# Retabling a hand-ordered attention and FFN kernel: DMA issue times and held buffers in the planner, and a masked product for the row maxima

## The chip, the cores and the metric

One core of one Trainium2 chip runs the whole program. The time is device microseconds of one launch; three runs of the kernel before gave 1584.69, 1585.31 and 1585.92 us, median 1585.31. One more execution was taken by the hardware profiler and took 1585.88 us.

## The reference

Four batches of 12416 rows with 128 channels go through an induced-set attention block, and each resulting row through a SwiGLU FFN (d_model 128, d_ff 1536). Everything is FP32.

```python
def mab(q, kv):
    s = scale * (q @ kv.transpose(0, 2, 1))
    s = s - s.max(-1, keepdims=True)
    a = np.exp(s)
    a /= a.sum(-1, keepdims=True) + 1e-09
    return a @ kv
h = mab(I, x)                 # 32 inducing points attend to all rows of the batch
x = mab(x, h)                 # every row attends to the 32 results
rms = np.sqrt(np.mean(x * x, axis=-1, keepdims=True) + 1e-06)
xn = x / rms * rms_g
g = xn @ w_gate
silu = g * (1.0 / (1.0 + np.exp(-g)))
val = xn @ w_val
return (silu * val @ w_out).astype(np.float32)
```

## The kernel before

**Slots.** A batch is cut into 7 sets of rows (`per`): six of four "units" (512 rows wide, the sixth 480) and a last one of a single unit of 256. That makes 25 units, and a unit has 12 blocks of d_ff. One pass through `slot` handles one block of one unit, so a batch has 300 slots and the kernel 1200. A slot is called k (0 to 299 in its batch) below. In a slot TensorE computes a gate product (L751) and a value product (L762) into PSUM banks, ScalarE applies silu (L759), and VectorE multiplies the two (L768).

**Three kinds of output product.** The product with `wo` is accumulated in `acc` at L688, and the letter of the slot in the table `letters` says how it is made. A "." slot uses full FP32, which the compiler issues as two matmuls (`acc<-u,wo`). An "s" or "d" slot splits the number in halves and makes three reduced-precision matmuls (L709, L711, L688: `u<-xn,xn`, `u<-xn,more`, `acc<-xn,more`; `project3`). The split itself costs other engines time. "s" (sums): one ScalarE pass (L733), one VectorE pass (L734), one GpSimd pass (L743). "d" (differences): two ScalarE passes (L737, L742) and two GpSimd passes (L738, L743), none on VectorE. The tiles that hold the halves are called `xn`, `sg`, `sv` or `xT` after the buffers that they borrow.

**Other work is threaded between the slots.** While batch b goes through its FFN, the attention of batch b+1 is computed: transposes, scores (L342) with their running maxima, exponentials, the sum over rows (`sum_h`, L396), then `stack` (L475) and `place` (L484). `stack(i)` multiplies the gate or value weights by the 32 attention results and leaves the rounded half in a tile `whi` (ScalarE, L478) and the rest in `wlo` (VectorE, L479). `place(i, k)` then copies three stripes of a half into the stacked weights `sg` or `sv` by DMA on the SP queue: k = 0 and 1 read `whi`, k = 2 and 3 read `wlo`. A "seam" prepares the attention weights of the next set of the current batch: `turn_a`, `square` (L521), `turn_z` (L527, L528), `scale`, `root`, `apply`, `turn_b`, `split` (L552, L555). `gather` (L567) then copies its result into the moving operand of the next unit by DMA, also on SP. So are the loads and the result's stores (L725).

**The order is written out by hand, in tables that a search found.** `letters` gives the kind of each slot; `places` the slot of each threaded step; `ordered` where the output products of earlier slots are issued (p: full, t: split); `banks` which of five PSUM banks each product takes; `workers` which of three buffers `work0` to `work2` each scratch tile takes; `holders` which of nine buffers each product tile takes. A scratch tile (`eT`, `z`, `aT`, `e`, `whi`, `wlo`) takes its buffer from the list in turn:

```python
def worker(shape, dtype, name):
    return work.tile(shape, dtype, name=name, tag=f"work{works.pop(0)}")
```

The buffer of `whi` or `wlo` is free for its next holder only when the last DMA of `place` that reads it has landed. The engines run their own instruction streams in order; SP too issues its DMAs in order.

**The maxima of batches 1 to 3.** After the scores of a batch, `max1` reduces seven maxima per partition to one, `max2` transposes them onto one partition, takes the maximum over the four quarters there and scales it, and `max3` spreads it back with a matmul and copies it to `nbias`. Batch 0 has its own start-up order (`first`), which does this by a masked product (L843, L851, L854).

Of the kernel before, what the change touches and what calls it, by code (L numbers as in the profile page):

```python
# [9 lines left out]
F32 = mybir.dt.float32  # L10
# [4 lines left out]
ALU = mybir.AluOpType  # L15
AX = mybir.AxisListType
PSUM = bass.MemoryType.PSUM

P = 128
R = 4  # L20
# [3 lines left out]
def kernel(  # L24
# [45 lines left out]
    nc = tc.nc  # L70
    B, N, C = x.shape
    m = inducing.shape[0]
# [10 lines left out]
    NS = len(per)  # L83
# [226 lines left out]
    def attention(b, load_next):  # L310
# [38 lines left out]
        def max1():  # L349
            mx = st["mx"] = small.tile([P, 1], F32, name="mx")  # L350
            nc.vector.reduce_max(out=mx[:], in_=st["gmx"][:], axis=AX.X)

        def max2():
            ps = bank()
            nc.tensor.transpose(ps[0:1, 0:P], st["mx"][:], ident[:])
            row = once.tile([1, m], F32, name="row")
            nc.vector.reduce_max(out=row[:], in_=ps[0:1, 0:P].rearrange("p (q m) -> p m q", m=m), axis=AX.X)
            row4 = st["row4"] = once.tile([P, P], F32, name="hg")[0:1, :].rearrange("p (q m) -> p q m", m=m)
            nc.vector.tensor_scalar_mul(out=row4, in0=row[:].unsqueeze(1).to_broadcast((1, R, m)), scalar1=-SCALE)

        def max3():
            ps = bank()
            nc.tensor.matmul(ps[:, 0:1], st["row4"].rearrange("p q m -> p (q m)"), ones[0:1, 0:1],
                             start=True, stop=True)
            nbias = st["nbias"] = small.tile([P, 1], F32, name="nbias")
            nc.vector.tensor_copy(out=nbias, in_=ps[:, 0:1])
# [681 lines left out]
    def given(b, k, u, j):  # L1048
# [4 lines left out]
        ..........................ss..ssdd.....sss.dsd..sd.ssdsds...d.sdddsd.....sdsdsss.s....sdsdsdss..ssss  # L1053
        dsdssd..dsd..ssdd...sd.sssd.ds....ss..dssd..sssdsssssd..ddsss.ssss..ssdsssssss..sss.ssssdd..ssssdsds
        sd..sssdd.s.ss..sssssssds...sss.ssssdd...ssssssd.s....ssd.d.ss..sssssd.d....ss.ss.sss...sssd.sdsdd..
        """,
        """
        d...dsssss..dssssdsd.s..dd.sd.sd.s..ssd.ss.dss..sds.sddsss..sdd...ds.d..ssss.d.dsd...ssssdsssd..ssd.
        sd.dss..sd.sssdsd...sssdsd.dsd..ss....dssd..ssssdssssd..ssdssssd.s..ssssdssssd...s.sdsssds..ssssdsds
        dd..sssssss..d..s.s.sssssd..sssssds.ds..ssssd.d.sd....s..dsssd..ssss.dsd....sss..sssss...s.sssdsdd..  # L1060
        """,
        """
        s.ssdsd.ds..ssssdsd.s...ss.s..dssd..sdsssds.ss..ssdsd..dd...sddss.dsds..s.s.sssds...sdsss.sdds..sssd
        ssdd.s..sssd.ssds...sssdssdsds.....s.d.sdd..sss.sssssd..sdssssdd.s..sss.dsssss..sssd.sssds..dsssdsss
        ds..ssd.sds.sd..sss.ssssss..d.sd.sssss..ssssssssds......dd..ss..sssd.ds.ss...s.sssssd...s.s.sd.dsd..
        """,
        """
        s.s.ssssd.s.sssssd.sds.sss...d..ssd..ssssdsd..ssss.ssssssdd..sss..sss..ssssssdsssss.s.sssd.s.sssss.s
        dsd.sssssd.s..ds.s.sssssd.s.d..ss.ssss.sd.ssssssssds.ssd..ssdsss..s..sss..sssdssssssdsd..ss.ssssss.s
        dsss.dsd.s..s.sssssss..sdsssss.sss.dss.sss.sssdsd.s.sdssss...s.sssss...sssdss.ds.sdsdsss..ssss...d..  # L1070
# [4 lines left out]
        0 0 1 1 2 2 2 2 3 3 4 4 4 5 6 6 7 7 8 8 9 9 10 10 11 11 11 11 12 12 13 13 13 13 13 14 16 17 18 16 19 18 20   # L1075
        21 16 20 21 21 22 22 24 23 25 24 27 24 24 27 27 24 28 29 24 28 29 30 30 31 32 32 32 34 34 35 35 35 35 35 39 
        41 39 42 43 44 45 47 49 51 54 54 54 55 58 59 62 62 55 65 65 62 66 64 67 66 70 71 66 70 73 73 77 75 77 77 79 
        85 81 84 85 86 89 87 89 90 92 92 96 97 97 96 100 103 103 104 108 108 109 101 116 109 111 111 110 116 110 118 
        123 116 129 120 132 123 132 134 135 136 136 142 146 147 148 148 154 148 160 161 151 162 153 156 159 168 163 
        168 171 171 174 175 178 191 192 196 197 198 198 199 208 199 203 205 210 212 208 215 197 208 216 216 218 202   # L1080
        213 202 215 206 215 208 215 211 221 227 215 221 218 225 230 233 227 230 239 239 233 239 247 248 239 239 250 
        245 250 251 254 254 255 256 257 256 256 256 260 263 266 262 269 268 268 271 277 273 275 275 280 281 285 287 
# [3 lines left out]
        0 0 6 12 4 13 18 13 20 18 18 21 19 24 26 30 27 30 36 35 35 36 39 39 42 46 48 54 50 52 54 58 60 60 66 62 53   # L1086
        63 59 66 63 70 65 69 71 74 72 87 75 81 76 83 79 79 87 82 93 96 97 100 103 118 100 102 108 107 100 114 103 
        104 111 118 115 122 130 119 132 126 133 134 135 136 136 142 146 147 148 146 156 149 160 161 151 162 153 159 
        164 169 164 166 171 178 174 175 180 180 185 195 196 198 198 198 204 201 202 202 211 214 204 209 198 204 209 
        214 219 202 215 202 215 208 204 209 215 212 218 221 216 221 215 220 226 234 227 233 237 239 233 233 240 246   # L1090
        239 244 246 245 249 251 254 254 255 256 257 256 256 256 257 263 266 262 269 269 268 270 271 272 272 275 277 
        281 281 283 287 293 299 
        """,
        """
        0 0 6 12 5 7 18 8 20 22 22 24 31 24 27 28 33 30 36 35 36 36 38 38 42 48 48 50 51 53 54 55 57 60 66 60 58 64 
        63 66 63 67 65 67 68 71 72 93 74 80 82 83 86 87 93 93 99 101 97 105 103 120 105 111 108 115 100 117 104 104 
        112 120 118 124 129 121 132 124 128 134 135 136 136 136 146 147 148 158 158 158 160 161 162 162 162 165 166 
        168 163 164 169 172 174 175 178 180 188 196 197 197 198 198 197 198 200 202 201 203 203 206 206 203 207 211 
        212 210 204 210 207 214 219 215 223 220 228 219 225 228 232 235 229 237 241 229 248 249 229 253 253 254 254 
        255 256 256 256 256 258 260 262 264 269 270 267 275 276 280 285 288   # L1100
        """,
        """
        2 4 6 19 21 21 25 26 31 35 37 53 58 58 60 62 76 78 81 103 108 108 110 113 125 129 131 156 158 158 161 161 
        173 177 181 199 206 206 209 215 218 225 227 250 253 253 257 257 264 269 271 
# [3 lines left out]
        ;;;,pp;,,,p;,p;,p;;,pp;;,pp;;;,pp,,,p;;,p;;,p;;,p;;,p;;;p;;;,p;;,pp;,pp;,pp;,tt;,pp;,,t;,t;;,p;;,tp;;,tp;;,p;,  # L1108
        pt;,tp;;,tp;;,t;;,tp;;,tp;;,tt;;,tt;;,tp;;,tp;;,t;,tp;;;,t;,tt;,pp;,t;;,pp;;,pt;;,t;,,p;;,t;,ppt;;,tt;;,tt;;,t
        p;;,tt;,,p;;,t;,pt;,t;;,pt;t;;,tp;;,tt;,p;;,t;,tt;;,tt;,tp;;,tp;,t;,t;;,tp;;,t;,tp;,t;,t;;,t;;,t;,p;;,t;,pp;,p  # L1110
        ;;,tp;,t;;,t;;,tt;,pt;,pp;,tt;,pp;,t;;,tp;,p;,t;;;t;;,t;,tp;;,tt;;t;t,t;,tt;,t;;,tp;;,,t;,t;;,t;,p;,pp;,t;,tt;
        ;,tt;;,tt;,p;,tp;,t;;t;,tt;,t;,t;;,t;;,tp;,t;;,t;,t;,tp;,t;,t;,,ttp;;;,tp;;,tp;,t;,t;,t;,t;,t;,t;;,tp;;,t;,tp;
        ,t;,t;;,tt;;,p;,t;,p;;,t;,t;,t;,tp;,t;,t;,tp;,t;,t;;,tt;;,p;;,t;,tp;;,t;,t;,tp;,t;,t;;,tt;;,t;,p;;,tp;,t;,t;,t
        ;;,tt;;,t;;,pp;,tt;,pp;,pp;,tp;;,tp;,t;;,p;,t;;,pp;,t;,t;,t;,tt;;t;,p;;,t;,p;;,tp;,t;,p;;,pp;,t;,t;,pt;;,t;;,t
        t;;,tp;,p;;,t;,t;,t;,pt;,t;;,pt;;,tp;,tp;,t;;,p;,tp;;,tp;;,t;,t;;;,tt;,t;,pt;;,tt;;,tt;;;p,p;;,t;;p;t,p;,t;,tp
        ;;,p;,t;,pt;;,t;,tt;;,pt;;,t;,pp;;,tt;;,tp;;,t;;,tp;,tt;;,tp;;,t;,tt;,tp;;;,t;;tt,t;;,tp;,p;,tt;;,tp;;,t;;,t;;
        ,pp;,p;,t;,pt;;,tp;,tt;,pp;;,t;;t;,tp;;,t;,p;,tt;,t;,tp;;,t;,t;,t;;,t;p;,tp;;,t;,tt;,tp;,t;,p;;,t;;,t;,t;,p;,t
        ;,pt;;,t;,t;,t;;,p;;,tp;;,t;,pt;,p;,t;,t;,t;;,p;,t;,tp;,tp;,tp;,tp;;,tp;,t;,t;,p;;,t;;t;;,tt;,p;;,tt;;t;t,tt;;
        ,tt;;,tp;;,t;;t,tt;;,tp;;,t;,t;,t;;,pp;,pt;,tp;,t;;;t;,tt;,t;;,t,,tt;;;,t;,p;,tp;;,t;,tp;,tp;,t;;,t;;,t;,tp;,t
        ;,pt;,t;,t;,tt;;,t;;,,t;;,t;,t;,t;,pt;,t;,t;,t;,pp;;,tt;;;,tp;;,tp;,p;;,tt;;pp,t;,t;,t;;;t;,tp;,t;,pt;,t;,t;;,  # L1120
        t;,t;;t,p;;,tp;,t;,t;,t;;,t;,t;;,t;,p;,t;;,pp;,tp;,tp;,tp;;;p,tp;,p;,t;,t;;,t;;,tp;,t;;,t;,tt;;,tp;,tp;;,t;,p;
        ;,pp;;,t;;,tp;,t;,t;,t;p,p;,t;;,t;;,t;,t;,p;,tt;;,tp;,t;;,tp;;,t;,tp;,tp;,pp;;,,tt;;,tt;;,t;,p;;,t;,p;,t;,tp;;
        ,t;,tt;;,tp;;,tt;;,tp;;,t;;,pp;;,t;,tt;,pp;;;,tt;;,tp;;,tp;,pt;;,tt;,t;;,tp;;,t;,,t;,t;;,t;,pp;,t;;,t;,tt;;,tp
        ;;,tp;;;,t;,pp;;,tt;,tt;,t;;,p;,p;,tp;;,t;,p;,t;,t;,pt;,tt;;,t;,t;;,p;,tt;;,pt;,pp;;,tt;;;t;,tt;;,t;,p;,t;,tp;
# [116 lines left out]
```

## Time and profile before

| what | value |
|---|---|
| median of three runs | 1585.31 us |
| profiled execution | 1585.88 us |
| its span, first to last instruction | 1584.0 us |
| TensorE busy | 1565.6 us |
| VectorE busy | 1458.7 us |
| ScalarE busy | 1300.0 us |
| GpSimd busy | 1428.0 us |
| granted TensorE clock | 0.999 |

The span lacks 1.9 us of the profiled execution's time. Busy times of different engines overlap. TensorE's busy time counts matmuls whose modelled ends overlap the next one's start, so what a matmul costs in a running stream is read from start to start, not from its own duration. The FFN slots run from about 52 us to the end, some 1.3 us each.

### The profile page before, as it was taken

The page shows a single profiled execution, that of the slowest core. Times are in us where ns is not written, and L with a number is a line of the kernel's source. Part 1 is how long each engine was busy: PE and PEld are TensorE (multiplying, and loading weights), DVE is VectorE, ACT ScalarE, POOL GpSimd, SP SyncE. Part 2 cuts the span into 40 slices and gives each one's busy share as a digit, 9 for nine tenths or more (in the row PEclk, how much of TensorE's full clock was granted, in tenths as well). Part 3 has the DMA queues.
Part 4 walks back from the last instruction along what each step waited for, and adds up shares of the span by engine and source line. Part 5 has one row for each costly group of instructions (what it writes and reads, how often), then busy time and mean ns, then how long its engine had stood idle before and what let it go on. Part 6 is the DMA issues. An engine that isn't in the chain of part 4 may idle for free.

```text
span 1584.0 us, 26071 instructions
## 1 busy us (share of the span) xinstructions
PE 1565.6 (99%) x7144; PEld 1106.6 (70%) x7144; DVE 1458.7 (92%) x2528; ACT 1300.0 (82%) x2491; POOL 1428.0 (90%) x1154
## 2 busy tenths in 40 slices
PE   8999999999999999999999999999999999999998
PEld 6566667767676666775677667676677777777777
DVE  6899989999999998988999999898999999999997
ACT  4588888878888789886888888978788888888887
POOL 1389999999899999998999999899989999999997
PEclk9999999999999999999999999999999999999999
DMA  6445524444353141634445314253221121221211
GB/s 256 111 75 95 101 46 104 92 90 73 65 91 67 30 96 33 134 82 80 72 70 90 57 33 90 61 131 76 45 39 37 32 39 34 37 38 34 40 37 29
DMA packets 389330, 112.57 MB, mean 71 GB/s; under 512 B 365088, under 2 KB 369728, under 8 KB 386624
## 3 DMA queue, kind: packets, MB, share of 16 engines
q1 hardware_dynamic: 388448, 110.82, 34.7%
q8 instruction: 57, 0.93, 0.3%
q14 instruction: 89, 0.73, 0.2%
q10 hardware_dynamic: 736, 0.08, 0.0%
HBM read 53.95 MB, written 27.00 MB: 51 GB/s over the span
## 4 chain that ended last, share of the span: by engine, by line
PE 93%; DVE 1%; ACT 1%; SPq 1%; issue 0%; DMA 0%; DVEq 0%; ACTq 0%
PE acc L688 31%; PE gv L751 17%; PE gv L762 17%; PE u L711 11%; PE u L709 11%; PE gv L342 2%; PE gv L521 1%; PE gv L396 1%; SPq L484 0%; DVE u L768 0%; ACT silu L759 0%; DMA sg<-wlo 0%; DVE gv L768 0%; DMA sg<-whi 0%; PE gv L475 0%
## 5 line engine op out<-in xcount | busy, mean ns | idle before, releaser
L743 POOL TENSOR_TENSOR xn<-xn,xn 128x512 fp32r<-128x512 f32 (+2 forms) x618 | 765.0, 1259 | 53.8 <-DVE xn L734 22.4
L759 ACT ACTIVATE silu<-gv 128x512 f32<-128x512 f32 (+2 forms) x1186 | 683.3, 587 | 143.4 <-PE gv L751 131.8
L762 PE MATMUL gv<-a,sv 128*128 128x512 f32 (+2 forms) x1188 | 572.0, 482 | 3.1 <-DVE wlo L479 1.8
L751 PE MATMUL gv<-a,sg 128*128 128x512 f32 (+2 forms) x1188 | 483.8, 408 | 0.7 <-DVE z L527 0.5
L768 DVE TENSOR_TENSOR gv<-silu,gv 128x512 f32<-128x512 f32 (+2 forms) x598 | 400.4, 674 | 39.3 <-PE gv L762 21.0
L768 DVE TENSOR_TENSOR u<-silu,gv 128x512 f32<-128x512 f32 (+2 forms) x588 | 381.8, 655 | 38.0 <-PE gv L762 16.7
L688 PE MATMUL acc<-u,wo 128*128 128x512 f32 (+2 forms) x782 | 379.4, 576 | 0.0
L751 PEld LDWEIGHTS gv<-a,sg 128*128 128x128 f32 x1188 | 223.5, 188 | 139.9 <-issue 33.2
L733 ACT ACTIVATE xn<-gv 128x512 fp32r<-128x512 f32 (+2 forms) x468 | 275.7, 589 | 55.0 <-DVE gv L768 39.9
L734 DVE SCALAR_TENSOR_TENSOR xn<-xn,gv 128x512 fp32r<-128x512 f32 (+2 forms) x468 | 309.2, 661 | 7.8 <-ACT xn L733 2.5
L762 PEld LDWEIGHTS gv<-a,sv 128*128 128x128 f32 x1188 | 223.7, 188 | 110.8 <-issue 25.8
L709 PE MATMUL u<-xn,xn 128*128 128x512 f32 (+2 forms) x598 | 240.3, 402 | 0.0
L688 PE MATMUL acc<-xn,more 128*128 128x512 f32 (+2 forms) x598 | 231.2, 387 | 0.0
L738 POOL TENSOR_TENSOR xn<-u,xn 128x512 fp32r<-128x512 f32 (+2 forms) x150 | 187.8, 1252 | 7.7 <-ACT xn L737 7.0
L688 PEld LDWEIGHTS acc<-u,wo 128*128 128x128 f32 x782 | 146.0, 188 | 47.6 <-issue 20.2
L709 PEld LDWEIGHTS u<-xn,xn 128*128 128x128 f32 x598 | 112.4, 188 | 29.2 <-issue 5.9
L743 POOL TENSOR_TENSOR sg<-sg 128x512 fp32r<-128x512 f32 (+1 forms) x96 | 123.5, 1286 | 6.9 <-DVE sg L734 2.4
L743 POOL TENSOR_TENSOR sv<-sv 128x512 fp32r<-128x512 f32 (+1 forms) x95 | 122.7, 1292 | 7.5 <-DVE sv L734 4.9
L688 PEld LDWEIGHTS acc<-xn,more 128*128 128x128 f32 x598 | 112.3, 188 | 23.3
L711 PE MATMUL u<-xn,more 128*128 128x512 f32 (+2 forms) x300 | 116.0, 387 | 0.0
L711 PE MATMUL u<-xn,xn 128*128 128x512 f32 (+2 forms) x298 | 114.8, 385 | 0.0
L737 ACT ACTIVATE xn<-u 128x512 fp32r<-128x512 f32 (+2 forms) x150 | 92.5, 617 | 10.7 <-DVE u L768 6.2
(220 smaller groups left out, 1912.9 us busy)
## 6 DMA issues: line engine op xcount, KB each, us to landing
out_dram<-o SPq DMA_DIRECT2D x320, 64.0 KB, 2.0
xT<-in_x_dram SPq DMA_DIRECT2D x60, 256.0 KB, 3.9
xn<-in_x_dram SPq DMA_DIRECT2D x60, 256.0 KB, 5.3
a<-hi SPq DMA_DIRECT2D x156, 64.0 KB, 2.0
a<-lo SPq DMA_DIRECT2D x156, 64.0 KB, 2.0
xn<-in_x_dram SPq DMA_DIRECT2D x5, 1024.0 KB, 10.2
xn<-w SPq DMA_DIRECT2D x18, 256.0 KB, 3.0
out_dram<-o SPq DMA_DIRECT2D x64, 60.0 KB, 2.0
```

The lines of the kernel that those rows point to most:

```text
L688: nc.tensor.matmul(acc[:, 0:T], lhsT, rhs, start=st["left"] == NJ, stop=st["left"] == 1)
L709: nc.tensor.matmul(ups[:, 0:T], weight_of(0, j), hi, start=st["k"] == nk, stop=False)
L711: nc.tensor.matmul(ups[:, 0:T], weight_of(1, j), lo, start=False, stop=not st["k"])
L733: nc.scalar.activation(hi, v, AF.Copy, scale=(1.0 - 2.0 ** -13) * 2.0 ** -12)
L734: nc.vector.scalar_tensor_tensor(out=lo, in0=hi.bitcast(F32), scalar=-4096.0, in1=v, op0=ALU.mult, op1=ALU.add)
L737: nc.scalar.activation(d, v, AF.Copy, scale=1.0 - 2.0 ** -13)
L738: nc.gpsimd.tensor_tensor(out=lo, in0=v, in1=d.bitcast(F32), op=ALU.subtract)
L743: nc.gpsimd.tensor_tensor(out=d, in0=hi.bitcast(F32), in1=lo.bitcast(F32), op=ALU.subtract)
L751: nc.tensor.matmul(g[:, 0:T], sg[:, ts(j, P)], a[:, 0:T], start=True, stop=True)
L759: nc.scalar.activation(sl[:, 0:T], g[:, 0:T], AF.Silu)
L762: nc.tensor.matmul(v[:, 0:T], sv[:, ts(j, P)], a[:, 0:T], start=True, stop=True)
L768: nc.vector.tensor_tensor(out=t[:, 0:T], in0=sl[:, 0:T], in1=v[:, 0:T], op=ALU.mult)
```

## The change

The masked product of batch 0 replaces the transposing path of batches 1 to 3: `max1` becomes one VectorE product of the seven maxima with a mask (28 columns), `max2` one matmul with `fold`, `max3` one minimum over 28 columns straight from PSUM. Two VectorE instructions and the transposing matmul go.

All six tables are replaced. The search that found them now models how long the SP queue takes to issue each DMA, and how long a DMA holds the buffer it reads.

```diff
         def max1():
-            mx = st["mx"] = small.tile([P, 1], F32, name="mx")
-            nc.vector.reduce_max(out=mx[:], in_=st["gmx"][:], axis=AX.X)
+            t = st["own"] = small.tile([P, R, NS], F32, name="owns")
+            nc.vector.tensor_tensor(out=t[:], in0=st["gmx"][:].unsqueeze(1).to_broadcast((P, R, NS)),
+                                    in1=quarter[:].unsqueeze(2).to_broadcast((P, R, NS)), op=ALU.mult)
 
         def max2():
-            ps = bank()
-            nc.tensor.transpose(ps[0:1, 0:P], st["mx"][:], ident[:])
-            row = once.tile([1, m], F32, name="row")
-            nc.vector.reduce_max(out=row[:], in_=ps[0:1, 0:P].rearrange("p (q m) -> p m q", m=m), axis=AX.X)
-            row4 = st["row4"] = once.tile([P, P], F32, name="hg")[0:1, :].rearrange("p (q m) -> p q m", m=m)
-            nc.vector.tensor_scalar_mul(out=row4, in0=row[:].unsqueeze(1).to_broadcast((1, R, m)), scalar1=-SCALE)
+            ps = st["max"] = bank()[:, 0:R * NS]
+            nc.tensor.matmul(ps, fold[:].rearrange("p q m -> p (q m)"), st["own"][:].rearrange("p q s -> p (q s)"),
+                             start=True, stop=True)
 
         def max3():
-            ps = bank()
-            nc.tensor.matmul(ps[:, 0:1], st["row4"].rearrange("p q m -> p (q m)"), ones[0:1, 0:1],
-                             start=True, stop=True)
             nbias = st["nbias"] = small.tile([P, 1], F32, name="nbias")
-            nc.vector.tensor_copy(out=nbias, in_=ps[:, 0:1])
+            nc.vector.tensor_reduce(out=nbias[:], in_=st["max"], axis=AX.X, op=ALU.min)
...
     letters = [
         """
-        ..........................ss..ssdd.....sss.dsd..sd.ssdsds...d.sdddsd.....sdsdsss.s....sdsdsdss..ssss
...
+        ..........................ss..s.dd...s.sssddss..ss.dsddsds...s.d.sssd....dssdss.ds..d.ssssdsdd..ssss
...
     workers = """
-        12012012012012010202010212012012012012102102102102010021021012012012012012012012012012012021021012012012012012
-        01201
+        12012012012012010201201202012012012012012012012010212012012012012012012012012012012021012012102102102102102102
+        10210
     """
```

`letters`, by batch (slots of kind s, d and "."):

| batch | before s / d / . | after s / d / . |
|---|---|---|
| 0 | 132 / 53 / 115 | 137 / 52 / 111 |
| 1 | 142 / 61 / 97 | 147 / 58 / 95 |
| 2 | 147 / 56 / 97 | 148 / 57 / 95 |
| 3 | 181 / 37 / 82 | 187 / 34 / 79 |
| sum | 602 / 207 / 391 | 619 / 201 / 380 |

By width of the unit, after less before: 512 rows s +17, d -9, "." -8; 480 rows s -1, d +3, "." -2; 256 rows s +1, d 0, "." -1.

`places` and `workers`, for the steps whose tiles the DMAs of `place` hold (slot k of the batch; in brackets the scratch buffer):

| batch | version | stack(0) [whi, wlo] | place(0, 0 to 3) | stack(1) [whi, wlo] | place(1, 0 to 3) | turn_z |
|---|---|---|---|---|---|---|
| 0 | before | 198 [2, 1] | 199, 199, 203, 205 | 208 [0, 1] | 215, 216, 216, 218 | 202 [2] |
| 0 | after | 198 [2, 0] | 202, 202, 202, 205 | 215 [0, 1] | 215, 215, 216, 219 | 211 [2] |
| 1 | before | 198 [0, 2] | 198, 201, 202, 202 | 204 [1, 2] | 209, 209, 214, 219 | 202 [0] |
| 1 | after | 196 [0, 1] | 196, 202, 202, 205 | 215 [1, 2] | 215, 215, 218, 218 | 211 [0] |
| 2 | before | 197 [1, 2] | 198, 198, 200, 202 | 203 [0, 1] | 206, 207, 211, 212 | 210 [0] |
| 2 | after | 198 [1, 2] | 200, 202, 203, 207 | 209 [1, 2] | 210, 212, 217, 217 | 217 [1] |

Around the row sums: in batch 1 `sum_h(2, 3)` and `turn_e(4)`, whose buffer is that of `turn_e(3)`, stand in slots 160 and 164 before and both in slot 160 after. In batch 2 `sum_h(2, 3)` stands in slot 160 in both; `square` and `turn_z` follow in slot 162 before and in slot 160 after.

## The prediction

> **What bounds the kernel now.** I read the page first: busy shares and the chain that ended last.
>
> ```profile
> PE 1565.6 (99%) x7144; PEld 1106.6 (70%) x7144; DVE 1458.7 (92%) x2528; ACT 1300.0 (82%) x2491; POOL 1428.0 (90%) x1154
> ...
> PE 93%; DVE 1%; ACT 1%; SPq 1%; issue 0%; DMA 0%; DVEq 0%; ACTq 0%
> ```
>
> TensorE is the bound. Nine tenths of the chain are its own matmuls, so two things shorten the kernel: less TensorE work, or fewer holes in it. VectorE and GpSimd are not far behind. Second, the windows, stage by stage (busy us of PE, PEld, DVE, ACT, POOL):
>
> ```profile
> 450.00:550.00 100.00, 100.00 (x397) 69.20 (x397) 94.61 (x160) 83.35 (x159) 96.97 (x77) 1.00 0.35 61
> 700.00:745.00 45.00, 42.32 (x183) 26.39 (x182) 38.31 (x64) 32.76 (x65) 37.73 (x30) 1.00 0.39 86
> 745.00:850.00 105.00, 105.00 (x448) 77.05 (x446) 97.65 (x174) 90.90 (x183) 98.40 (x88) 1.00 0.45 76
> 1400.00:1500.00 100.00, 100.00 (x394) 73.72 (x393) 96.56 (x160) 85.97 (x163) 98.46 (x77) 1.00 0.20 36
> ```
>
> In most stretches PE has no hole that this view can show; in 700 to 745 it has 2.7 us of them, with every other engine slacker too: something outside the engines was late. Third, the waits that a DMA ended, after 60 us:
>
> ```profile
> DVE z L527 <- DMA sg<-whi: 5.3, 2, 2.9
> DVE wlo L479 <- DMA sg<-wlo: 1.8, 1, 1.8
> ```
>
> Three waits. The chain shows one of them in batch 0:
>
> ```profile
> 327.35 0.60 SPq L484
> ...
> 327.99 3.00 DMA sg<-whi
> ...
> 331.31 0.67 DVE z L527
> ...
> 332.02 0.50 PE gv L762
> ...
> 332.75 0.23 PE u L709
> 332.98 0.23 PE u L711
> ```
>
> `turn_z` writes `z` into the buffer that held `whi`, and six copies of `place`, about 0.6 us of SP's time each, still read it; the last takes 3.0 us. VectorE stands, PE's next product has no bank. Fourth, the timeline at the three places says what PE loses:
>
> ```profile
> 330.41 0.40 PE L751 MATMUL gv<-a,sg 128*128 128x512 f32 x1
> ...
> 332.02 0.50 PE L762 MATMUL gv<-a,sv 128*128 128x512 f32 x1 [1.21 <-DVE z L527]
> ...
> 720.00 0.50 PE L751 MATMUL gv<-a,sg 128*128 128x512 f32 x1
> ...
> 722.27 0.49 PE L762 MATMUL gv<-a,sv 128*128 128x512 f32 x1 [1.77 <-DVE wlo L479]
> ...
> 722.89 0.50 PE L751 MATMUL gv<-a,sg 128*128 128x512 f32 x1
> ```
>
> A reduced product costs 0.23 us start to start (the L709 and L711 pieces of the chain). So PE loses 332.02 - 330.41 - 0.23 = 1.4 us, 722.27 - 720.00 - 0.23 = 2.0, and 722.89 - 722.27 - 0.23 = 0.4. At 717.29 a `z` wait costs 0.8 more (the eight L342 that start at 715.52 take 0.93, half of the chain's 1.85 for sixteen; the next starts at 717.29). Together 4.7 us. About 0.7 us more is lost near 345 and 1.0 near 740, where the chain leaves PE for VectorE and ScalarE again, catching up.
>
> **The change, part by part**, against the profiled execution's 1585.9 us (span 1584.0 and 1.9 around it; the median of the runs, 1585.3, is 0.6 lower).
>
> *Fewer full-precision products.* The chain of the whole run has:
>
> ```profile
> 69.51 1.72 PE acc L688 x4
> ...
> 399.75 1.61 PE acc L688 x4
> ```
>
> Four of them take 1.72 us at 512 rows, so a "." slot (two) costs 0.86, and 0.80 at 480 rows (1.61). A split slot costs 3 x 0.23 = 0.69, or 0.65 at 480 rows in proportion. Eight fewer at 512, two at 480 and one at 256 (about half) save 8 x 0.17 + 2 x 0.15 + 0.08 = 1.7 us. [...] The measured pair is 0.86, so I keep 1.7.
>
> *What the split slots load elsewhere.* VectorE: 17 more "s" at 512, one fewer at 480, one more at 256, with rows of 0.677, 0.643 and 0.417: +11.3 us. GpSimd: 17 x 1.297 - 9 x (1.301 + 1.297), the 480-row slots -1.2 + 7.3, the 256-row +0.7: +5.5. ScalarE: about +2. These lie beside PE. Their cover: VectorE is busy 1418 of the 1523 us from 55 to 1578 and would be busy 1427 of some 1517, 94% after 93%; GpSimd 1418 becomes 1423, 94% after 93%. Cover remains, though thin: with it gone, each VectorE microsecond would be one of the kernel.
>
> *The maxima.* Per batch VectorE loses 0.15 (L351), 0.27 (L357), 0.2 to 1.3 (L359) and 0.15 (L366), and gains a product and a reduction like L843 and L854, 0.17 each. That is 0.4 to 1.5 us off VectorE. PE loses a transposing product of 0.27 and two of 0.26 and gains a pair like L851's 0.26: about 0.2 each in a running stream, 0.5 us over three batches. The new `max3` follows `max2` within the same slot in batches 0 to 2, so VectorE may wait one short matmul, with one multiply behind it. The exponentials stay in slot 134 with a slot or more in hand. Total -0.5.
>
> *The held buffers.* A slot is 1.29 us (387 us for the 300 of batch 1). In batches 0 and 1 the last copy that reads `whi` is issued at slot 202 and `turn_z` takes that buffer at slot 211, 11.6 us later. Six issues of 0.6 and the 3.0 of the trace are 6.6 us: clear by 5. Batch 1's second `stack` no longer takes the `wlo` buffer of the first. So all three waits go: -4.7 us, and of the 1.7 us of catching up afterwards I count half, -0.8. What is late next is the work that was moved.
>
> *New tight places.* (a) Batch 2: the second `stack` at slot 209 takes both buffers of the first. The copy that frees `wlo` stands at slot 207, behind the `gather` of slot 206 on SP; that gather's buffer is free when PE leaves slot 203, so four gather issues (2.4 us) and three of `place` (1.8) end near slot 207, plus landing. Then `turn_z` at 217 takes the second `whi`, whose last copy stands at 212 behind four stores of slot 211. [...] Bounds: nothing, to twice the 2.4 us lost at 720; I take 0.5. (b) Batch 1, slot 160: `turn_e(4)` waits for `sum_h(2, 3)` of the same slot (1.89 us for 64 products in the chain), with the next multiply queued behind it; and batch 2, slot 160, `turn_z` waits for `sum_h` and a 0.86 us `square`. VectorE does its 0.68 multiply meanwhile, so up to 1.2 and 2.1 us idle. The nearest row, 331.31, cost PE half of VectorE's idle time, and VectorE usually trails PE; between 0 and 1.7, I take 0.7. (c) The last product is now a split one, so ScalarE's copy of `u` (about 0.4 at 256 rows) stands before the final add: 0 to 0.4, I take 0.2.
>
> The order moves no more work onto SP: the copies are the same, they stand later. Split products are issued on average 6.7 slots after their slot in both tables, so no slack was sold for the extra eleven.
>
> Sum: -1.7 - 0.5 - 4.7 - 0.8 + 0.5 + 0.7 + 0.2 = -6.3; 1585.9 - 6.3 = 1579.6 profiled, 1579.0 as a median.
>
> **The rivals.** *The waits move instead of going* (0.17). The retabled steps meet other holders, as in (a), or the four `scores2` now bunched in slot 20 of batch 0 and the three behind `stack(1)` in slot 215 of batch 1 cost what the old waits did. For it: the tables before also came from a search, and kept three waits. Against: the buffers' distances, counted above. Only the products and the maxima are left: 1585.3 - 2.2 = 1583.1; with half of the waits back, 1580.5.
>
> *VectorE becomes the bound* (0.11), the case on the other side. The multiply of every slot stands on VectorE, and PE needs its bank back. [...] For it: 96.6% in 1400 to 1500, where batch 3 gets six more "s" slots. Against: where VectorE showed 96.6%, PE had no hole. If all is paid, 1585.3 + 11.3 - 6.9 (products, maxima and waits, as above) = 1589.7; the kernel is slower than before once more than about 7 us of it are paid.
>
> **How the numbers follow.** The main case has 0.72, and its bounds give 1574 (all catching up gone, no new wait) to 1583. A difference of 0.2%, 3.2 us, is about what a measurement of this kernel can tell from none. Faster by more, under 1582.1: 0.70 of the main case and 0.07 of the first rival, 0.77. Within: 0.02, 0.10 and 0.02, 0.14. Slower, over 1588.5: 0.09. The range 1573 to 1586 holds the main case and the first rival up to a microsecond above the time before, leaving out the second rival and the tails.
>
> **What would show it.** Right: the waits list has no VectorE wait ended by a copy into `sg` or `sv`; the chain stays on PE through the slots around 200 to 217 of batches 0 and 1; 760 matmuls `acc<-u,wo` instead of 782; L734 up by 17; PE's hole in 700 to 745 gone. Wrong: new waits of `z` or `wlo` near the same slots of batch 2 (first rival), or long chain stretches on VectorE multiplies in batch 3 (second). A time above 1586 would refute the accounting of the held buffers.

## The result, and the profile after

| | before | after |
|---|---|---|
| median, runs side by side | 1585.31 us (1584.31 to 1587.03) | 1577.88 us (1577.82 to 1578.06) |
| profiled execution | 1585.88 us | 1578.04 us |
| span | 1584.0 us | 1576.1 us |

The ratio is 0.9953, with a 95% interval of 0.9938 to 0.9967: 7.4 us faster, and the interval lies wholly beyond the 0.2% that the prediction took for the limit of measurement. It had said 1579.0.

The page of the changed kernel, busy shares and chain:

```profile
PE 1560.8 (99%) x7152; PEld 1110.4 (70%) x7152; DVE 1464.1 (93%) x2539; ACT 1300.6 (83%) x2496; POOL 1432.6 (91%) x1159
PE 96%; DVE 2%; DMA 1%; ACT 0%; issue 0%; POOL 0%; SPq 0%; DVEq 0%; ACTq 0%
```

TensorE has eight matmuls more and is busy 4.8 us less; its share of the chain went from 93% to 96%. VectorE has 5.4 us more to do, in a kernel that is 7.9 us shorter in its span. From here on, lines behind the maxima carry numbers lower by 5 than before (L751 became L746, L762 L757, L768 L763, L734 L729, L484 L479).

The windows (busy us of PE, PEld, DVE, ACT, POOL, then clock, DMA share, GB/s): batch 1 as a whole, and 45 us that hold the place of the hole of before.

```profile
448.00:835.00 387.00, 387.00 (x1768) 276.00 (x1767) 362.39 (x626) 327.09 (x630) 367.44 (x298) 1.00 0.41 77
694.00:739.00 45.00, 45.00 (x202) 30.60 (x201) 43.23 (x72) 36.27 (x72) 41.84 (x33) 1.00 0.43 88
```

The hole is gone: PE is busy for all of the 45 us, with 202 matmuls in them instead of 183. VectorE does 43.2 us in them instead of 38.3. After 60 us the waits list holds no VectorE wait that a DMA ended, and by the landings in the trace none hides behind another name. The timeline of batch 0 shows `z` arriving with its buffer long free, no idle time in front of it:

```profile
341.25 0.69 DVE L763 TENSOR_TENSOR gv<-silu,gv 128x512 f32<-128x512 f32 x1
341.93 0.66 DVE L522 TENSOR_TENSOR z<-gv,eT 128x480 f32<-128x480 f32 x1
```

One sign of the prediction did not hold: in batch 0 the chain does not stay on PE. In slots 204 to 208 it runs over VectorE for 3.7 us, as the ends of this stretch show.

```profile
331.58 0.52 DVE u L763
...
335.28 0.50 PE gv L746
```

VectorE is busy for all of the 8 us from 329 to 337, and by its rows TensorE loses about 0.5 us there.

The groups count 760 matmuls `acc<-u,wo`, and L729 ran 619 times where L734 had run 602.

One new wait is in the timeline of the first slots:

```profile
54.83 0.39 PE L757 MATMUL gv<-a,sv 128*128 128x512 f32 x1
56.29 0.47 PE L746 MATMUL gv<-a,sg 128*128 128x512 f32 x1 [1.07 <-DMA a<-lo]
56.60 1.88 PE L683 MATMUL acc<-u,wo 128*128 128x512 f32 x4
```

Before, four matmuls of full-precision products stood in front of the product that needs the gathered operand, and covered its landing (the same place of before):

```profile
54.75 1.88 PE L688 MATMUL acc<-u,wo 128*128 128x512 f32 x4
56.06 0.80 PE L762 MATMUL gv<-a,sv 128*128 128x512 f32 x1
```

To say where the time went I compare TensorE's rows slot by slot: between the gate products of the same two slots, the change of the elapsed time less the change of the matmuls' cost there (start-to-start rows). By this measure the change lost 1.9 us in the first 31 slots of batch 0, won 2.2 in slots 190 to 230 of batch 0, 1.3 from there to slot 190 of batch 1, 4.3 from there to slot 100 of batch 2, and 1.2 in slots 190 to 240 of batch 2, lost 1.3 in slots 40 to 80 of batch 3 and won 0.8 behind them. That is a measure of stretches, and it does not say what in a stretch did it: there the waits went, but the order of products and steps was new too. The experiments separate these.

### The profile page after: what moved, and what is told of

Read it like the earlier page. It is cut to its first block, busy times and chain, and to the rows that moved or that the text cites. A ratio compares the mean times of both kernels' runs of the same rounds, so it can differ in the third digit from the quotient of the medians.

```text
span 1576.1 us, 26147 instructions
## 1 busy us (share of the span) xinstructions
PE 1560.8 (99%) x7152; PEld 1110.4 (70%) x7152; DVE 1464.1 (93%) x2539; ACT 1300.6 (83%) x2496; POOL 1432.6 (91%) x1159
## 4 chain that ended last, share of the span: by engine, by line
PE 96%; DVE 2%; DMA 1%; ACT 0%; issue 0%; POOL 0%; SPq 0%; DVEq 0%; ACTq 0%
PE acc L683 32%; PE gv L746 18%; PE gv L757 17%; PE u L704 12%; PE u L706 12%; PE gv L342 3%; PE gv L516 1%; PE gv L391 1%; PE gv L820 1%; DMA xn<-in_x_dram 1%; PE gv L470 0%; DMA a<-lo 0%; ACT silu L754 0%; DVE u L763 0%; PE gv L484 0%
## 5 line engine op out<-in xcount | busy, mean ns | idle before, releaser
L738 POOL TENSOR_TENSOR xn<-xn,xn 128x512 fp32r<-128x512 f32 (+2 forms) x627 | 776.0, 1257 | 48.0 <-DVE xn L729 14.8
L757 PE MATMUL gv<-a,sv 128*128 128x512 f32 (+2 forms) x1188 | 567.0, 478 | 0.0
L746 PE MATMUL gv<-a,sg 128*128 128x512 f32 (+2 forms) x1188 | 482.0, 406 | 1.3 <-DMA a<-lo 1.1
L763 DVE TENSOR_TENSOR gv<-silu,gv 128x512 f32<-128x512 f32 (+2 forms) x616 | 412.3, 674 | 34.4 <-PE gv L757 12.6
L763 DVE TENSOR_TENSOR u<-silu,gv 128x512 f32<-128x512 f32 (+2 forms) x570 | 370.6, 657 | 35.7 <-PE gv L757 17.1
L683 PE MATMUL acc<-u,wo 128*128 128x512 f32 (+2 forms) x760 | 370.0, 577 | 0.0
L729 DVE SCALAR_TENSOR_TENSOR xn<-xn,gv 128x512 fp32r<-128x512 f32 (+2 forms) x472 | 312.9, 663 | 9.3 <-ACT xn L728 4.4
L746 PEld LDWEIGHTS gv<-a,sg 128*128 128x128 f32 x1188 | 223.8, 188 | 133.2 <-issue 32.1
L757 PEld LDWEIGHTS gv<-a,sv 128*128 128x128 f32 x1188 | 224.0, 189 | 106.6 <-issue 27.2
L733 POOL TENSOR_TENSOR xn<-u,xn 128x512 fp32r<-128x512 f32 (+2 forms) x155 | 192.9, 1245 | 6.3 <-ACT xn L732 6.2
L683 PEld LDWEIGHTS acc<-u,wo 128*128 128x128 f32 x760 | 142.2, 189 | 43.3 <-issue 17.2
L738 POOL TENSOR_TENSOR sg<-sg 128x512 fp32r<-128x512 f32 (+2 forms) x97 | 124.5, 1283 | 4.8 <-DVE sg L729 1.8
L732 ACT ACTIVATE xn<-u 128x512 fp32r<-128x512 f32 (+2 forms) x155 | 95.8, 618 | 12.7 <-DVE u L763 5.6
```

What stands on the lines that cost most here:

```text
L683: nc.tensor.matmul(acc[:, 0:T], lhsT, rhs, start=st["left"] == NJ, stop=st["left"] == 1)
L729: nc.vector.scalar_tensor_tensor(out=lo, in0=hi.bitcast(F32), scalar=-4096.0, in1=v, op0=ALU.mult, op1=ALU.add)
L732: nc.scalar.activation(d, v, AF.Copy, scale=1.0 - 2.0 ** -13)
L733: nc.gpsimd.tensor_tensor(out=lo, in0=v, in1=d.bitcast(F32), op=ALU.subtract)
L738: nc.gpsimd.tensor_tensor(out=d, in0=hi.bitcast(F32), in1=lo.bitcast(F32), op=ALU.subtract)
L746: nc.tensor.matmul(g[:, 0:T], sg[:, ts(j, P)], a[:, 0:T], start=True, stop=True)
```

## The experiments

Every kernel was run beside the kernel before on the same chip; the medians of the kernel before were 1585.4 to 1585.8 us. Comparisons with the changed kernel's 1577.88 us are between different series of runs.

**One: the waits taken away by moving steps later.** The tables of before, with only these steps moved:

```diff
 batch 0, set 5
-square 202, turn_z 202, scale 206, root 208, apply 211
+square 207, turn_z 207, scale 209, root 210, apply 213
 batch 1, set 5, and stack(1)
-square 202, turn_z 202, stack(1) 204, scale 208, root 209, apply 212
+square 207, turn_z 207, stack(1) 209, scale 210, root 211, apply 213
```

> The kernel before, with only the steps moved that take a buffer which the copies of place still read: in batch 0 square and turn_z from slot 202 to 207 (and scale, root and apply behind them to 209, 210 and 213), in batch 1 the same and the second stack from slot 204 to 209. Letters, buffers and maxima are as before. Theory (the waits on held buffers were the loss): the holes of TensorE at slots 190 to 220 of batch 0 and of batch 1 go, 2.2 and 4.2 us in the comparison of the two traces, so 1579 to 1580.5 us. Rival (the waits only show where time is lost that another engine would have lost anyway, and the gain came from the rest of the tables): within 1 us of 1585.3.

Measured: 1584.18 us, ratio 0.9992 (0.9983 to 1.0001). The theory missed. No VectorE wait on a copy was left in batches 0 and 1, but TensorE won only 1.2 us in batch 0 and 0.3 in batch 1, since other holes had opened there:

```profile
720.65 1.07 PE L521 MATMUL gv<-eT,gram 128*128 128x480 f32 x2 [0.65 <-DVE xn L734]
...
727.37 0.51 PE L762 MATMUL gv<-a,sv 128*128 128x512 f32 x1 [0.35 <-DVE wlo L479]
```

The moved `square` now waits for a bank that VectorE frees late. Moving five steps to take away one wait changes more than the wait, so this run could not decide; a cleaner removal comes below.

**Two: the maxima alone.** The kernel before with the new `max1`, `max2` and `max3`; `max2` stands in the slot and the bank of `max3`.

> The kernel before with only the maxima of batches 1 to 3 made by the masked product (max2 stands in the slot of max3, in the PSUM bank that max3 had). All tables otherwise as before. Theory (only TensorE's own time counts, two or three short matmuls less): -0.5 us, 1584.8. Rival (VectorE's time is saved one to one, 0.4 to 1.5 us a batch): 1582 to 1583.5. Third: the product waits in the stream and costs as much as it saves, 1585.3.

Measured: 1583.41 us, ratio 0.9988 (0.9979 to 0.9997), 1.9 us. That is near the rival's "one to one"; the prediction's 0.5 stands at the edge of the interval. VectorE's busy time fell by 1.7 us and TensorE's by 2.1. But not all of this belongs to the maxima. By TensorE's rows slots 100 to 150, which hold them, give about 0, 0.4 and 0.5 us in the three batches. Another 0.5 is a shorter wait on a copy (the second `wlo` of batch 1 waited 1.3 us instead of 1.8), and 0.4 another one in batch 2 (0.3 instead of 0.95, described under seven). The rest is spread in smaller pieces. Why the copies were in better time was not traced, and `max2` also stands 9, 7 and 4 slots later than before.

**Three and four: the first slots.** The changed kernel with the tables of before for slots 0 to 30 of batch 0, and for slots 0 to 13. The places of output products around the gather, for slots 3 to 6 (groups within a slot are split by commas):

```diff
-slot 3: none     slot 4: ,pp,,p    slot 5: none   slot 6: ,pp
+slot 3: ,pp      slot 4: ,,,p      slot 5: ,p     slot 6: ,p
```

> The changed kernel, with the tables of the kernel before for slots 0 to 30 of batch 0 (places, order of products, banks and buffers; the letters of these slots are the same in both). Theory (the change loses 1.9 us of TensorE's time there, 1.4 at slot 3 where the gate product waits for a gather, the rest where four scores are bunched in slot 20, and nothing gives it back): 1576.0 us. Rival (the loss is taken up by slack later, or is chance of one profile): 1577.9.

> The changed kernel, with the tables of the kernel before for slots 0 to 13 of batch 0 only, where four output matmuls again stand ahead of the gate product that reads the gathered operand. Theory: that wait of 1.1 to 1.4 us goes and about 0.7 of it remains saved at slot 16, as the comparison of the traces has it: 1576.5 to 1577.2. Rival (the gather's landing, 3.9 us here, varies from run to run, or the bunch in slot 20 hides it): 1577.9.

Measured: 1577.76 us (ratio 0.995, 0.9937 to 0.9962) and 1577.32 (0.9947, 0.9935 to 0.996). The wait on `a<-lo` was gone in both, and TensorE was 1.3 to 1.4 us ahead of the changed kernel at slot 10; 0.5 and about 1.0 us of that lasted. As device time it is 0.1 and 0.6 us, within the intervals. The second is the fastest kernel measured here, by less than could be told from no difference. The size of the wait changes from one execution to the next: with the same tables in these slots run ten stood 1.3 us at this product, and run five only 0.26:

```profile
55.48 0.47 PE L746 MATMUL gv<-a,sg 128*128 128x512 f32 x1 [0.26 <-DMA a<-lo]
```

**Five: copies started later.**

```diff
 changed kernel, batches 0 and 1
-place(0, 0 to 3): 202, 202, 202, 205 and 196, 202, 202, 205
+place(0, 0 to 3): 208, 208, 209, 210 in both
```

> The changed kernel with only its copies of the value and gate weights made late again: in batches 0 and 1 the four groups of copies of the first product start at slots 208, 208, 209 and 210 instead of 196 to 205. No instruction of PE, VectorE, ScalarE or GpSimd moves. z of the next set (slot 211) takes the buffer that the first two groups read; six copies at 0.59 us each on SP's queue and about 3 us to the landing put the release near slot 213, so z should wait some 2 to 3 us in each of the two batches, as long as it waited before the change (1.4 and 2.0). Theory one, the waits themselves were what the change saved: TensorE loses most of it, 2 to 4 us in all, 1580 to 1582, with a hole in TensorE's row at slots 211 to 216 of both batches. Theory two, the waits were a small part and the new order of products and steps the larger: the output products that stand ready cover the wait, under 1.5 us in all, 1577.9 to 1579.3.

Measured: 1578.46 us, ratio 0.995 (0.9937 to 0.9962). It agrees with theory two and proves nothing: there was no wait to cover. SP's timeline of batch 0 says why.

```profile
330.20 0.54 SPq L562 DMA_DIRECT2D a<-hi  x1
...
332.75 3.70 SPq L479 DMA_DIRECT2D sg<-whi  x6
336.54 3.70 SPq L479 DMA_DIRECT2D sg<-wlo  x6
```

The slot of a `place` did not set when its copy started here; it only set what stood ahead of it on SP's queue. These copies went out right behind the gather, 1.8 us ahead of slot 208 (its gate product starts at 334.57), and `whi` was free before `z` came at 341.2. My expectation had counted from the slot.

**Six: `z` in place.** The kernel before, and `z` of set 5 in batches 0 and 1 written over the tile that it is made from. Nothing moves; the second `whi` of batch 1 gets the buffer left over.

```diff
-z = st["z"] = worker([P, 512], F32, "z")[:, 0:n * m].rearrange("p (t m) -> p t m", m=m)
+z = st["eT"] if b < 2 and s == 5 else worker([P, 512], F32, "z")
+z = st["z"] = z[:, 0:n * m].rearrange("p (t m) -> p t m", m=m)
```

> The kernel before with z written over the transposed scores that it is made from (set 5 of batches 0 and 1), so that z takes no scratch buffer and waits for no copy; to keep it free of a standstill, the high half of batch 1's second weight product takes the buffer that z had. No step, product or bank moves. The waits of 1.4 us at 330 and of 2.0 at 717 must be gone, the 0.4 at 722.9 stays. Theory one (waits themselves): 1585.3 less 1.4 and 2.0 and half of the catching-up, 1581.5 to 1583. Theory two (the waits were a small part): TensorE runs into the next thing that the order has late, as in the kernel with the steps moved, and at most 1.2 us come: 1584.1 to 1585.3.

Measured: 1584.56 us, ratio 0.999 (0.9982 to 0.9999). The total fits theory two, the rows do not. In batch 0, TensorE won 2.2 us in slots 190 to 230, with the same matmuls in the same order: what the changed kernel wins there. In batch 1 it lost 0.7, for VectorE's wait had gone on to the next holder (the waits list, microseconds in total, times, longest):

```profile
DVE wlo L479 <- DMA sg<-wlo: 3.6, 1, 3.6
```

VectorE reached the second `wlo` earlier and waited for the same landing, 3.6 us instead of 1.8. A wait of one step was covering part of the next one. The wait is not all of the loss: behind TensorE's hole, from 721.5 to 724.1, reduced products stood 0.43 us apart instead of 0.23, as they do at a granted clock of 0.50 in this run's first slots (the last section has the window). By these rows that took about 1.5 us, so with 0.23 batch 1 would have won some 0.8 (an estimate).

**Seven: both waits of batch 1 taken away.** As six, and one step later in batch 1; its second `whi` keeps its buffer.

```diff
-stack(1) 204
+stack(1) 209
```

> The kernel before with z in place in both batches, as in the run that won 2.2 us in batch 0 by TensorE's rows but in batch 1 only let the wait go on to the low half of the second weight product (1.8 us before, 3.6 there); now that product stands five slots later in batch 1 (209 instead of 204), so that no wait on a copy is left in either batch. Theory one (the waits themselves are what the change saved): 2.2 us in batch 0 and some 3 to 4 in batch 1, 1579.5 to 1581.5. Theory two (taking waits away pays only where products and steps are fitted anew): the 2.2 us of batch 0 and less than 1 in batch 1, 1582 to 1583.5.

Measured: 1581.12 us, ratio 0.997 (0.9959 to 0.998), 4.3 us faster. Theory one had 1579.5 to 1581.5. Slots 190 to 230 give 2.2 us in batch 0 and 2.4 in batch 1, with TensorE's matmuls otherwise in the order of before. Half a microsecond comes back in batch 2, where a wait has grown. The kernel before's row stands first:

```profile
1113.41 0.66 DVE L527 TENSOR_TENSOR z<-gv,eT 128x480 f32<-128x480 f32 x1 [0.95 <-PE gv L751]
```

```profile
1108.88 0.66 DVE L528 TENSOR_TENSOR z<-gv,eT 128x480 f32<-128x480 f32 x1 [1.38 <-DMA sv<-whi]
```

Here TensorE shows a hole of 0.91 us at 1109.59. So the kernel before had a fourth wait on a copy, which the prediction's list of three lacks: the profile puts it down to a gate product. But `square`, whose product `z` reads, had started at 1111.03, and in the trace the last copy that reads this `whi` lands at 1113.29, 0.12 us ahead of `z`, as it does here (1108.76). It cost TensorE about 0.7 us (its next product starts at 1114.12, the one ahead of it at 1113.23). In run seven VectorE and TensorE reached this place 5.0 us earlier than before, the copy 4.5, for one issue of the gather ahead of it on SP took longer:

```profile
1107.59 1.77 SPq L567 DMA_DIRECT2D a<-hi  x1
```

```profile
1102.64 2.20 SPq L568 DMA_DIRECT2D a<-hi  x1
```

**Eight: the wait put back into the changed kernel.** As five, and `z` in the buffer of the low half, whose copies are later.

```diff
 batch 0
-turn_z [2], stack(1) [0, 1], turn_b [2]
+turn_z [0], stack(1) [2, 1], turn_b [0]
 batch 1
-turn_z [0], stack(1) [1, 2], turn_b [0]
+turn_z [1], stack(1) [0, 2], turn_b [1]
```

> The kernel with the copies started late, in which no wait arose, once more with the waits made sure: z (slot 211, batches 0 and 1) takes the buffer of the LOW half, whose copies were issued until 340.2 and 723.9 there, while z came at 341.2 and 722.8; the buffers of the second weight product and of the following transpose are swapped to match. No instruction moves on any engine. With some 2.3 us from the last issue to the landing z should wait about 1.3 us in batch 0 and 3.6 in batch 1, near what it waited before the change (2.9 and 2.3 on VectorE's own row). Theory one (VectorE's waits reach TensorE): 3 to 5 us lost, at slots 211 to 216 of both batches, 1580.5 to 1583. Theory two (the new order covers such waits): under 1.5 us, 1577.9 to 1579.3.

Measured: 1581.70 us, ratio 0.9973 (0.9963 to 0.9984), by the medians 3.8 us over the changed kernel. In batch 0, `z` idled 0.5 us and TensorE's rows show nothing lost. In batch 1 (VectorE's row, then TensorE's):

```profile
726.22 0.66 DVE L522 TENSOR_TENSOR z<-gv,eT 128x480 f32<-128x480 f32 x1 [2.86 <-DMA sg<-wlo]
```

```profile
726.93 0.50 PE L746 MATMUL gv<-a,sg 128*128 128x512 f32 x1 [2.39 <-DVE z L522]
```

2.9 us of idle VectorE cost TensorE 4.2 in slots 210 to 220, and nowhere else did the two kernels differ by more than 0.4. Of these the hole itself is 2.6 us (the product ahead of it starts at 724.14; 726.93 - 724.14 - 0.23). Behind it the granted clock (the column after POOL's) was half:

```profile
727.60:731.00 3.40, 3.40 (x8) 1.83 (x6) 3.37 (x7) 1.72 (x3) 2.10 (x2) 0.50 0.09 13
```

From the gate product behind the hole to the one behind the next scores TensorE took 7.9 us (726.93 to 734.80); the changed kernel takes 6.1 for the same matmuls (724.60 to 730.74). That is the other 1.7. So in the new order, too, a held buffer by itself brings such a loss: a hole, and in this execution half clock behind it.

**Nine: the parts added.** Seven and two together, on the tables of before.

> The kernel before with the two parts that can be done without new tables together: the waits taken away as in the run beside this one, and the maxima of batches 1 to 3 by the masked product (1.9 us faster alone). If they add up, it is 1.5 to 2.2 us under the run beside it: 1577.5 to 1580 by theory one, 1580 to 1582 by theory two. The changed kernel's 22 further split products (1.7 us of TensorE's work) are not in it.

Measured: 1579.07 us, ratio 0.9959 (0.9947 to 0.9972), 6.4 us faster, 2.05 under seven: the parts add up. But by TensorE's rows 0.8 of what it wins over seven lies in slots 200 to 230 of batch 2, where `z` stands 0.54 us instead of 1.38. This kernel lacks the 11 further split products (the expectation's 22 are their matmuls) and the search's order, and the changed kernel is 1 us or so away, with intervals that overlap.

**Ten: 40 products of batch 3 in full precision again.** In `letters` and the matching places of `ordered` (31 "s" and 9 "d" become "."), with a holder added for each of the 31.

> The changed kernel with 40 of batch 3's output products, 31 with sums and 9 with differences, made in full precision again (letters only; all else in its place). By TensorE's rows each costs 0.86 us instead of three times 0.231, 0.17 us more, so 40 cost 6.8 us if TensorE sets the time: 1584.7 (1583.5 to 1585.5). The rival, VectorE or GpSimd set the time in the last batch: VectorE has 31 times 0.67, 21 us, less to do, GpSimd 62 us less and ScalarE about 35 us less, so it is as fast or faster, 1577.9 or less.

Measured: 1586.75 us, ratio 1.0005 (0.9996 to 1.0014), 8.9 us over the changed kernel and above the expected range. The matmuls' rows give 6.7 of it and new holes of TensorE 2.6, whose cause was not traced. VectorE, with 1449.5 us busy instead of 1464.1, and GpSimd, with 1372.7 instead of 1432.6, bought nothing: TensorE, not their load, sets the time in batch 3.

**Eleven: 33 "d" made "s".** In `letters`; the holders that these slots no longer need are dropped.

> The changed kernel with 33 of its products with differences (every sixth, over all batches) made with sums: VectorE gets 33 times 0.67, 22 us, more, GpSimd about 43 us and ScalarE 20 us less; TensorE's work is unchanged. If VectorE has room beside TensorE (93% busy, 1464 of 1576 us), it costs 0 to 3 us: 1577.9 to 1581. If VectorE were the bound, the 22 us come through nearly one to one: 1590 to 1600.

Measured: 1626.95 us, ratio 1.0258 (1.0244 to 1.0272): 49 us, so both expectations missed. VectorE's busy time rose by the 21 us that were meant (1485.5), but it is idle for longer, 91% busy. The waits list of TensorE has new entries, absent from the changed kernel's:

```profile
PE gv L746 <- DVE xn L729: 11.8, 10, 2.7
PE gv L757 <- DVE xn L729: 10.3, 9, 1.7
PE gv L757 <- DVE sg L729: 5.8, 4, 1.8
PE gv L746 <- DVE sv L729: 3.5, 2, 2.5
```

An "s" slot keeps its product in the PSUM bank of the value matmul until VectorE's L729 has read it (the page's L763 `gv<-silu,gv`), while a "d" slot moves it to SBUF at once (`u<-silu,gv`). The bank's next user stands in `banks` where a "d" had freed it in time. So this run measured a held buffer again, in PSUM: 1.5 us for each changed letter, and 31 us of direct waits. A lower clock is in it as well: behind 2.46 us of idle TensorE, which end at 132.87, reduced products stood 0.43 us apart, and the mean granted clock of the profiled execution is 0.994 where the changed kernel has 1.0, worth some 10 us of its 1625.5 (an estimate, 0.006 of the span). The run says nothing clean about VectorE's load alone.

## Why the prediction was right

*TensorE as the bound, holes as the prey*: right. Run ten costs what the matmuls cost, and more; PE's share of the chain rose.

*The held buffers, -4.7*: right in mechanism, and in size with some luck. Runs six and seven, which change no product, give 2.2 us in batch 0 and 2.4 in batch 1, together 4.6, and run eight takes 4.2 away again in batch 1, 2.6 of them as the hole itself. The prediction had 1.4 for batch 0 and 3.2 for batch 1; the split between them was off. It also missed the fourth wait, in batch 2, worth about 0.7 us to TensorE and gone in the changed kernel: it took the releasers of the waits list as they stood.

*Half of the catching up, -0.8*: not seen as an extra. The 2.2 of batch 0 holds some of it (1.4 direct), batch 1 holds less than the direct waits. That VectorE's idle time reaches TensorE at half, as in the row at 331.31, failed as a rule: in run eight 0.5 us cost nothing, and 2.9 left a hole of 2.6 with 1.7 of half clock behind it.

*The maxima, -0.5*: too small, by how much is open. Alone they gave 1.9 us, added to the waits 2.05. Of these, 0.9 and 0.8 are shorter waits on copies, which the prediction did not count here; the slots around the maxima give 0.9. So about 1 us is the maxima's own. The prediction counted only PE's 0.2 us a batch and put VectorE's time at nothing. VectorE's busy time fell by 0.6 us a batch, inside the 0.4 to 1.5 that it was to lose; that this came through is a likely reading, and not shown.

*Fewer full-precision products, -1.7*: right as a price. The changed kernel's own step has no run to itself; forty letters of batch 3 cost 0.17 each by the rows, as predicted for 512 columns, and 0.22 with the holes that they opened.

*New tight places, +1.4*: about 0.2 came where they were put. (a) shows no wait on a copy in the changed kernel: its 0.5 no run shows, and the copies of `place` landed 2.0 us after their issue at the median in both kernels, the slowest after 3.8 before and 5.0 in the changed one. At (b) VectorE idles 0.5 us at most and TensorE has no hole. (c) came as taken: the final add waits for ScalarE's copy and starts 0.3 us after the last matmul's modelled end, where it started 0.1 us after it before.

```profile
1571.45 0.42 DVE L691 TENSOR_TENSOR o<-acc,o 128x256 f32<-128x256 f32 x1 [1.89 <-ACT o L709]
```

The mechanism of (a) exists, in the tables of before: it is the wait of batch 2 that grew in run seven. What else was lost lay elsewhere: up to 1.9 us in the first 31 slots and 1.3 in batch 3, slots 40 to 80. The prediction had read `places` and `workers` slot by slot, but not `ordered`, where the cover of the first gather had moved. Its size is open: the runs with the old first slots gain 0.1 and 0.6 us. What lost the 1.3 in batch 3 was not tried.

*Cover on VectorE*: enough at 93% over the whole, but not in each place, as the 0.5 us in slots 204 to 208 of batch 0 show. VectorE's busy time rose by 5.4 us, where the prediction had about 9. The last rival, VectorE as the bound, did not come; its price, each further microsecond of VectorE paid by the kernel, is not refuted for larger loads, since run eleven mixed it with held banks.

The sum by the runs: waits and maxima together -6.4 (run nine), products -1.7 as priced, the tail +0.2, so -7.9 against a measured -7.4 (ratio's interval 5.2 to 9.8). The new order as a whole is worth about nothing on top, which no run isolates. For the first of these the prediction had -6.0, with about 1 us too much for the waits and their catching up as run seven has them, and too little for the maxima: that they nearly cancel is luck. The rest of its distance is 1.2 us of new waits that did not come where it put them.

## What to carry to other kernels

A buffer read by a DMA is a resource like an engine: in run eight the next holder stood 2.9 us for it. Count when its last reader lands from the order of the issuing queue, not from the place in the program (in run five the copies went out 1.8 us ahead of their slot), and look at who takes the buffer next. A list of waits names one releaser each, so compare the start of the waiting operation with the landing too (in batch 2 they lie 0.12 us apart, where the list names a gate product). Where an operation can write over its own input, no holder is needed at all (run six, 2.2 us in batch 0). Removing one wait can uncover the next in the same queue (3.6 us instead of 1.8 in run six), so take away a whole chain of them before judging, and change nothing else in that run. On an engine that is 93% busy and frees TensorE's banks, time that lies beside TensorE may not be free (the maxima gave about 1 us where TensorE's own time had 0.5; that VectorE made the difference was not shown), and should get a price of its own.

## What the runs showed that was not expected

*The clock in the first slots.* TensorE idles 1.79 us at about 50 us in the traces of both kernels and of runs three and four, and 1.8 in run eleven's. In four of the 13 profiled executions (runs six, eight, nine and eleven) a stretch that had begun by 52.6 us ran at half clock, for 3.4 us by the windows of runs six, eight and nine; in the others reduced products stood 0.23 us apart in the first slots (here the window of run six):

```profile
52.00:54.00 2.00, 2.00 (x5) 1.61 (x6) 0.75 (x2) 1.39 (x3) 0.00 (x0) 0.50 1.03 329
```

Reduced products stood 0.43 us apart there instead of 0.23 (52.38, 52.81, 53.23 in its timeline). It cost run six about 1.2 us: the first full-precision products start at 55.91, those of the kernel before at 54.75. A difference of a microsecond at the start of two profiles is therefore no finding by itself.

*Idle time that grows on the way.* Behind the first slots the rows show the same three times, each behind a hole of TensorE: 2.11 us of idle time up to 720.27 in run six, with reduced products 0.43 us apart from 721.49 on; 2.39 up to 726.93 in run eight, with the granted clock at 0.50 from 727.60 to 731.00; 2.46 up to 132.87 in run eleven, with 0.43 from 133.46 on. The kernel before's 1.77 us up to 722.27 had no such stretch behind them (clock 1.00 from 722.3 to 728), nor had the 1.79 at about 50 us in either kernel. So in run eight the wait cost the hole's own 2.6 us and 1.7 more, half of the stretch's 3.4.

In the 56 executions of the kernel before beside these experiments the time goes with the mean granted clock: 1584.1 to 1585.8 us in the 19 at 1.0, and 1586.6 to 1588.5 in the ten at 0.997. That its waits set off such stretches in those ten would fit this, but they were not profiled. The five runs of the changed kernel lie within 0.3 us of each other.
